# A residual quantiser between two convolutions: one add, the turned one-hots, the updates and the code choice done in another way

## The chip, the cores and the metric

The kernel runs on one core of one Trainium2 chip. The metric is the device time of one execution in microseconds (us), the median of several runs. Five engines work side by side, each in the order in which its instructions were written, and wait for each other by semaphores: PE (matrix multiply), DVE (vector), ACT (activation), POOL, and SP, which issues transfers. Transfers run on 16 DMA engines that all queues share.

## The reference

The input x has B=2 sequences of T=16000 tokens with D=512 channels in bf16. The reference convolves along time with three taps per channel, applies SiLU, quantises with four codebooks of eight words each, and convolves the quantised signal again:

```python
z = sum over i of xp[:, i:i+T, :] * dw_enc[i]
z = silu(z)
res, q = z, 0
for s in range(4):
    cb = codebooks[s]                      # 8 words of 512
    d2 = |res|^2 - 2 res.cb^T + |cb|^2
    sel = cb[d2.argmin(-1)]                # the first of equal words
    q, res = q + sel, res - sel
y = sum over i of qp[:, i:i+T, :] * dw_dec[i]
```

## The kernel before

**Tiles.** The 32000 tokens are 128 partitions of S=250 consecutive tokens each. A group g is the 128 tokens at place g of every partition. The groups are cut into 16 chunks, SIZES (line 25): one of 12, fourteen of 16, one of 14. In a chunk, the channels lie on the partitions in KT=4 blocks of 128, and the tokens of up to 16 groups on the free axis, so that a full tile is 128x2048.

**Front** (load, lines 348 to 381; front, lines 383 to 467). Chunk 0 is read as rows and turned by PE; every other chunk is read by 18 transposing transfers from SP, one per group with a neighbour on each side (line 358), into one of two XT buffers. For each of the four channel blocks, DVE makes three products (product, line 410: Z, T, T), adds them in two steps (total, line 418), then SiLU is exp (ACT, line 422), plus one (DVE, 426), log (ACT, 430), exp (ACT, 433), and a product into RES (DVE, 438). There are 3 Z and 3 T buffers; Z is held from the first product to line 438. In total and add_up (lines 413 and 443) a branch for k <= DMA_ADDS issues the add as an accumulating DMA from POOL instead; DMA_ADDS is 0, so it is not taken.

**Stage s of 4** (stage, lines 469 to 621). PE scores: per bank of up to 6 groups, a mask and 8 small matmuls a group (lines 489 and 494) leave in PSUM the products of each token with the words and with all tokens; DVE takes the largest of the masked diagonal as the norm (502) and copies the dot products (505). Six small DVE steps choose the word: with_norm (522), distance (528), least (532), marks (536, which words equal the least), first (541, the greatest of the marks weighted by preset ranks in KEY, line 271), and onehot (549). PE turns the one-hots by four transposes (turn, 559) and ACT copies them to OHT (turned, 566). Then RES is updated: for each of the four channel blocks and each pair of quarters j, j+1 of the chunk, either PE selects the words (SEL, 584) and DVE adds them (subtract, 596), a quarter of 512 columns at a time, or PE sums RES and the words (NEW, 601 and 584) and ACT copies 1024 columns back (keep, 607). ON_DVE (line 28) says how many of the four blocks go to DVE in stages 0 to 2: 1, 1, 2, and 2, 2, 3 in the last three chunks. Stage 3 updates nothing.

**Finish** (lines 664 to 692). The second convolution is matmuls of OHT with words already multiplied by the taps (Y, 633), copied by ACT (639) to YSB and stored from SP (643), four groups at a time.

**PSUM.** Of the eight banks, the pool psG has two (scores), psD two single ones (SEL), psA two double ones (NEW, Y, the turned one-hots and set-up work).

**The order.** No engine chooses at run time. Plan (line 40) takes every step with its engine, an assumed time on the engine (hold), a time to its result (delay), what it needs, a due time and the buffers that it takes and gives back. It plays the steps through once while the program is built: on each assumed engine, of the steps that are ready and have their buffers, the one due first is emitted. That fixes the order on every engine. Chunks are due 56 assumed us apart per 16 groups (PERIOD), the stages of one chunk 0.9 of that apart, the blocks of a front 0.3. SP's loads are assumed to hold 1.4 and land after 2.2; an add by DMA to hold 1.2 + 1.8 f and land after 7.5, f being the chunk's size over 16. The stores are planned on an engine of their own, OUT, but in the program they stand in SP's queue among the loads. Where PE would be idle, a warming matmul (line 313) is put in.

Of the kernel before, what the change touches and what calls it, by code (L numbers as in the profile page):

```python
# [18 lines left out]
GC = 16  # L19
J = 4  # L20
GB = 6
HT = 64
# [97 lines left out]
def kernel(  # L120
# [61 lines left out]
    for i in range(KT):  # L182
# [4 lines left out]
    plan = Plan({"XT": 2, "Z": ZB, "T": TB, "E": EB, "LN": LNB, "Y": YB, "psG": 2, "psD": 2, "psA": 2, "RES": 3, "KEY": 3,  # L187
                 "OH": 3})

    RESB = []  # L190
# [34 lines left out]
    def code_norms():  # L225
        ONES = const.tile([NC, P], BF16, name="ONES")
        nc.vector.memset(ONES, 1.0)
        JUNK = const.tile([NC, D], BF16, name="JUNK")
        GF = const.tile([NC, 1], F32, name="GF")
        nc.vector.tensor_tensor_reduce(out=JUNK, in0=CB4[0:NC, :], in1=CB4[0:NC, :], scale=1.0, scalar=0.0,  # L230
                                       op0=ALU.mult, op1=ALU.add, accum_out=GF)
        GBB = const.tile([NC, 1], BF16, name="GBB")
        nc.vector.tensor_copy(GBB, GF)
        GBF = const.tile([NC, 1], F32, name="GBF")
        nc.vector.tensor_copy(GBF, GBB)
        DIAG = const.tile([NC, NC], BF16, name="DIAG")
        nc.vector.tensor_scalar(out=DIAG, in0=IDENT[0:NC, 0:NC], scalar1=GBF, scalar2=None, op0=ALU.mult)
        psg = psD.tile([P, 512], F32, name="ps_g", tag="psd")
        nc.tensor.matmul(psg[:, 0:NC], lhsT=ONES, rhs=DIAG, start=True, stop=True)
        nc.vector.tensor_copy(GPOS, psg[:, 0:NC])  # L240


    MASK = const.tile([P, GB, HT], BF16, name="MASK")
# [23 lines left out]
        free["OH"].append(t)  # L267

    def presets(n):
        for c in range(C):  # L270
            nc.vector.memset(KEYS[n][1][:, :, c, 0], float(C - c))
        nc.vector.memset(OHB[n], 0.0)

    KEYS, OHB = list(free["KEY"]), list(free["OH"])

# [16 lines left out]
        nc.vector.tensor_tensor(out=t, in0=t, in1=CB4, op=ALU.mult)  # L292

    early = -4.0 * PERIOD
    codes = [plan.add("DVE", 0.3, 0.5, [], early, code_words)]
    codes[0] = plan.add("DVE", 1.2, 1.4, codes, early + 2.0, lambda: code_columns(RESB[0]))
    scored = [plan.add("DVE", 2.4, 2.6, [], early + 1.0, mask), plan.add("DVE", 1.9, 2.1, [], early + 1.0, code_norms)]
# [50 lines left out]
    def load(st, org):  # L348
        g0, G, GP = st["g0"], st["G"], st["GP"]
        done = []  # L350
        if g0 == 0:
            load_rows(st, org)
            return

        def one(n):
            if n == 0:
                st["XT"] = xpool.tile([P, KT, GC + 2, P], BF16, name="XT")
# [23 lines left out]
        st["loaded"] = [done[-1], st.get("edge")]  # L381

    def front(st, org):
        n, G, MB = st["n"], st["GP"], st["MB"]
# [18 lines left out]
        def block(i):  # L403
# [44 lines left out]
            hold, delay = dve(0.67), dve(0.67) + 0.1  # L448
            z = plan.add("DVE", hold, delay, st["loaded"], due, lambda: product(0), take=("Z",))
            t = plan.add("DVE", hold, delay, st["loaded"], due, lambda: product(1), take=("T",))  # L450
            z = add_up(1, [z, t])
            t = plan.add("DVE", hold, delay, st["loaded"], due, lambda: product(2), take=("T",), give=("XT",) if i == KT - 1 else ())
# [16 lines left out]
    def stage(st, s, due):  # L469
# [53 lines left out]
                                    op=ALU.add)  # L523

        def distance():
            u["D2"] = small.tile([P, GC, C], BF16, name="D2")
            g2 = GPOS[:, C * s:C * s + C].rearrange("p (o c) -> p o c", o=1).to_broadcast([P, G, C])
            nc.vector.tensor_tensor(out=u["D2"][:, 0:G, :], in0=u["V"][:, 0:G, :], in1=g2, op=ALU.add)

        def least():  # L530
            u["M"] = small.tile([P, GC], BF16, name="M")
            nc.vector.tensor_reduce(out=u["M"][:, 0:G], in_=u["D2"][:, 0:G, :], axis=AX.X, op=ALU.min)

        def marks():
            u["KEY"] = free["KEY"].pop(0)
            nc.vector.tensor_tensor(out=u["KEY"][1][:, 0:G, :, 1], in0=u["D2"][:, 0:G, :],
                                    in1=u["M"][:, 0:G].to_broadcast([P, G, C]), op=ALU.is_equal)

        def first():
            u["M2"] = small.tile([P, GC], F32, name="M2")  # L540
            nc.vector.tensor_reduce(out=u["M2"][:, 0:G], in_=u["KEY"][0][:, 0:G, :], axis=AX.X, op=ALU.max)

        def onehot():
            if s == 0:
                st["OH"] = free["OH"].pop(0)
            dst = st["OH"][:, 0:G, s, :].rearrange("p (m j) c -> p j m c", j=J)
            key = u["KEY"][0][:, 0:G, :].rearrange("p (j m) c -> p j m c", m=MB)
            best = u["M2"][:, 0:G].rearrange("p (j m) -> p j m", m=MB).to_broadcast([P, J, MB, C])
            nc.vector.tensor_tensor(out=dst, in0=key, in1=best, op=ALU.is_equal)
            free["KEY"].append(u["KEY"])  # L550
            if s == Nq - 1 and G > st["G"]:
# [12 lines left out]
        def turned():  # L564
            u["OHT"] = ohpool.tile([P, GC // J, P], BF16, name="OHT", tag="oht" if s < Nq - 1 else "fin")
            nc.scalar.activation(u["OHT"][:, 0:MB, :], u["ps"][:, 0:W].rearrange("p (m t) -> p m t", t=P), ACT.Copy)  # L566
            st["OHT"] = u["OHT"]

        due += 0.01 * PERIOD
        t = plan.add("DVE", 0.2, 0.33, maxima, due, with_norm)  # L570
        t = plan.add("DVE", 0.15, 0.26, [t], due, distance)
        t = plan.add("DVE", 0.2, 0.33, [t], due, least)
        t = plan.add("DVE", 0.2, 0.33, [t] + preset[0:3], due, marks, take=("KEY",))
        t = plan.add("DVE", 0.2, 0.33, [t], due, first)
# [12 lines left out]
        def tokens(i, j, count):  # L587
            return st["RES"][:, i, 2 * j * MB:2 * (j + count) * MB, LC:LC + HT]

        def chosen(i, j):  # L590
            u["SEL", i, j] = psD.tile([P, 512], F32, name="SEL", tag="psd")
            select(u["SEL", i, j][:, 0:W], i, j, True)

        def subtract(i, j):
            old = tokens(i, j, 1)
            nc.vector.tensor_tensor(out=old, in0=old, in1=u["SEL", i, j][:, 0:W].rearrange("p (m t) -> p m t", t=HT), op=ALU.add)  # L596

        def rest(i, j):
            NEW = u["NEW", i, j] = psA.tile([P, 2, 512], F32, name="NEW", tag="psa")
# [3 lines left out]
                select(NEW[:, h, 0:W], i, j + h, False)  # L603

        def keep(i, j):
            old = tokens(i, j, 2).rearrange("p (h m) t -> p h m t", h=2)
            nc.scalar.activation(old, u["NEW", i, j][:, :, 0:W].rearrange("p h (m t) -> p h m t", t=HT), ACT.Copy)  # L607

        due += 0.01 * PERIOD
        for j in range(0, J, 2):  # L610
            for i in range(KT):
                if i < on_dve[s]:
                    for k in (j, j + 1):
                        c = plan.add("PE", 0.25 * f, 0.25 * f + 0.2, [t, words], due, lambda i=i, k=k: chosen(i, k), take=("psD",))
                        st["new"][i, k] = plan.add("DVE", 0.1 + 0.53 * f, 0.2 + 0.53 * f, [c] + seen, due,
                                                   lambda i=i, k=k: subtract(i, k), give=("psD",))
# [117 lines left out]
```

## Time and profile before

| | us |
|---|---|
| median of 3 runs | 830.86 |
| the runs | 828.19, 830.86, 836.56 |
| span of the profiled execution (first to last instruction) | 824.6 |
| its own time | not given beside the span; the median is 6.3 above it |
| busy PE, DVE, ACT, POOL in it | 653.2, 752.2, 717.8, 7.4 |
| DMA engines busy, mean share by the SP queue | 35.8% |
| granted PE clock, mean | 0.912 |

One execution is profiled; busy times are unions of the engine's instructions. A group's line in the profile gives the line of the kernel, the engine, the operation, what it writes and reads with shapes, the count, the busy time of the group, the mean duration of one in ns, and the idle time of the engine just before, with what ended it. Instructions of one engine overlap at their ends, so that the mean duration is longer than the distance from one start to the next.

### The profile page before, as it was taken

How to read it: one execution, taken by the hardware profiler on the slowest of the kernel's cores; microseconds unless marked ns; L12 is line 12 of the kernel's file. 1: busy time of each engine (PE TensorE's matmuls, PEld its weight loads, DVE VectorE, ACT ScalarE, POOL GpSimd, SP SyncE). 2: the span in 40 equal slices, each digit the busy share in tenths (PEclk: the TensorE clock that was granted, in tenths of full speed). 3: DMA queues.
4: the chain of work that ended last, by engine and by line, in shares of the span. 5: the costliest groups of instructions: out<-in, count | busy, mean ns of one | idle time of the engine just before them, and what ended most of it. 6: DMA issues, size and time to landing. Idle time of an engine off the chain costs nothing.

```text
span 824.6 us, 23407 instructions
## 1 busy us (share of the span) xinstructions
PE 653.2 (79%) x10289; PEld 314.0 (38%) x10289; DVE 752.2 (91%) x1584; ACT 717.8 (87%) x623; POOL 7.4 (1%) x17
## 2 busy tenths in 40 slices
PE   3047697898788879868888788779898888989995
PEld 2023333443343444424444244334434434334442
DVE  5987999999999999999999999998989999988871
ACT  2659788898999999999999999998989999886564
POOL 1100000000000000000000000000000000000000
PEclk9566877798998999999999999998979999989998
DMA  7442422152452635253716353451615301111132
GB/s 172 48 98 61 86 52 59 34 117 39 109 111 53 136 70 99 59 119 72 160 53 148 59 117 72 89 138 42 135 44 110 98 36 70 52 79 52 79 143 114
DMA packets 156207, 71.82 MB, mean 87 GB/s; under 512 B 147401, under 2 KB 147786, under 8 KB 155978
## 3 DMA queue, kind: packets, MB, share of 16 engines
q1 hardware_dynamic: 155152, 69.64, 35.8%
q8 instruction: 80, 1.31, 0.7%
q0 software_dynamic: 672, 0.43, 0.5%
q10 hardware_dynamic: 282, 0.26, 0.1%
q14 instruction: 21, 0.17, 0.1%
HBM read 2.39 MB, written 32.77 MB: 43 GB/s over the span
## 4 chain that ended last, share of the span: by engine, by line
ACT 41%; DVE 31%; PE 22%; issue 3%; DMA 2%; ACTq 0%; DVEq 0%
ACT RES L607 11%; ACT LN L430 8%; ACT YSB L639 7%; ACT E L422 7%; ACT E L433 7%; DVE Z L418 6%; DVE RES L596 6%; PE PS L494 6%; PE NEW L601 5%; DVE TR L502 4%; DVE RES L438 3%; DVE T L410 3%; PE NEW L584 3%; PE Y L633 3%; PE SEL L584 2%
## 5 line engine op out<-in xcount | busy, mean ns | idle before, releaser
L607 ACT ACTIVATE RES<-NEW 128x1024 bf16<-128x1024 f32 (+1 forms) x238 | 234.7, 1037 | 29.2 <-PE NEW L584 24.6
L494 PE MATMUL PS<-RES 128*64 128x80 bf16 (+1 forms) x8064 | 189.3, 208 | 27.4 <-DVE RES L438 26.7
L596 DVE TENSOR_TENSOR RES<-RES,SEL 128x512 bf16<-128x512 bf16 (+1 forms) x292 | 185.7, 674 | 19.6 <-PE SEL L584 19.2
L494 PEld LDWEIGHTS <-RES 128*64 128x64 bf16 x8064 | 165.6, 119 | 75.5 <-issue 36.8
L601 PE MATMUL NEW<-RES,IDENT 128*128 128x512 bf16 (+1 forms) x476 | 154.2, 408 | 30.8 <-ACT RES L607 27.0
L418 DVE TENSOR_TENSOR Z<-Z,T 128x2048 bf16<-128x2048 bf16 (+1 forms) x128 | 153.7, 1200 | 0.0
L639 ACT ACTIVATE YSB<-Y 128x1024 bf16<-128x1024 f32 (+1 forms) x126 | 128.1, 1042 | 17.8 <-PE Y L633 12.0
L422 ACT ACTIVATE E<-Z 128x2048 bf16<-128x2048 bf16 (+1 forms) x64 | 122.6, 1916 | 16.2 <-DVE Z L418 16.2
L430 ACT ACTIVATE LN<-E 128x2048 f32<-128x2048 bf16 (+1 forms) x64 | 122.3, 1913 | 8.0 <-DVE E L426 8.0
L433 ACT ACTIVATE E<-LN 128x2048 bf16<-128x2048 f32 (+1 forms) x64 | 122.8, 1920 | 0.2
L502 DVE TENSOR_REDUCE TR<-PS 128x5 bf16<-128x320 f32 (+1 forms) x188 | 95.5, 510 | 17.9 <-PE PS L494 17.5
L633 PE MATMUL Y<-A,OHT 128*128 128x512 bf16 x249 | 86.4, 390 | 30.5 <-ACT RES L607 17.2
L584 PE MATMUL SEL<-OHT,CBN 32*128 32x512 bf16 (+1 forms) x292 | 84.4, 397 | 27.3 <-ACT OHT L566 15.5
L584 PE MATMUL NEW<-OHT,CBN 32*128 32x512 bf16 (+1 forms) x476 | 97.8, 407 | 0.0
L410 DVE TENSOR_SCALAR T<-XT,WENC 128x2048 bf16<-128x2048 bf16 (+1 forms) x128 | 93.5, 740 | 0.0
L584 PEld LDWEIGHTS <-CBN 32*128 32x128 bf16 x768 | 35.2, 92 | 149.9 <-issue 144.4
L438 DVE TENSOR_TENSOR RES<-Z,E 128x2048 bf16<-128x2048 bf16 (+1 forms) x64 | 76.9, 1202 | 6.6 <-ACT E L433 4.0
L601 PEld LDWEIGHTS <-IDENT 128*128 128x128 bf16 x476 | 33.7, 99 | 106.0 <-issue 103.8
L489 PE MATMUL PS<-MASK,IDENT 128*128 128x320 bf16 (+1 forms) x188 | 62.6, 333 | 10.4 <-DVE PR L505 10.1
L633 PEld LDWEIGHTS <-OHT 128*128 128x128 bf16 x373 | 32.5, 98 | 70.2 <-issue 46.9
L566 ACT ACTIVATE OHT<-ps_oh 128x512 bf16<-128x512 bf16 (+1 forms) x64 | 39.7, 623 | 17.0 <-PE ps_oh L559 16.9
L633 PE MATMUL Y<-B,OHT 128*128 128x512 bf16 x124 | 47.4, 383 | 0.1
(73 smaller groups left out, 370.9 us busy)
## 6 DMA issues: line engine op xcount, KB each, us to landing
out_dram<-YSB SPq DMA_DIRECT2D x61, 512.0 KB, 3.2
XT<-in_x_dram SPq DMA_TRANSPOSE x267, 2.8
RES<-in_x_dram SPq DMA_DIRECT2D x1, 1664.0 KB, 6.9
out_dram<-YSB SPq DMA_DIRECT2D x1, 384.0 KB, 2.3
out_dram<-YSB SPq DMA_DIRECT2D x1, 256.0 KB
A<-in_dw_dec_dram POOLq DMA_DIRECT2D x2, 96.0 KB, 5.3
CB<-in_codebooks_dram ACTq DMA_DIRECT2D x1, 128.0 KB
A<-in_dw_dec_dram POOLq DMA_DIRECT2D x2, 64.0 KB, 4.8
```

The source lines that it names most:

```text
L418: nc.vector.tensor_tensor(out=z, in0=z, in1=t, op=ALU.add)
L422: nc.scalar.activation(u["E"][:, 0:G, :], u["Z"][:, 0:G, :], ACT.Exp, scale=-1.0)
L430: nc.scalar.activation(u["LN"][:, 0:G, :], u["E"][:, 0:G, :], ACT.Ln)
L433: nc.scalar.activation(u["E"][:, 0:G, :], u["LN"][:, 0:G, :], ACT.Exp, scale=-1.0)
L494: nc.tensor.matmul(V[h * HT:(h + 1) * HT, r, :], lhsT=half[:, LC:LC + HT], rhs=half[:, lo:hi], start=False, stop=(i == KT - 1), skip_group ...
L502: nc.vector.tensor_reduce(out=u["TR"][:, q:q + m], in_=u["V", q][:, :, own:own + HT], axis=AX.X, op=ALU.max)
L584: nc.tensor.matmul(ps, lhsT=CBN[s][rows, i * P:(i + 1) * P], rhs=u["OHT"][rows, 0:MB, :], start=start, stop=True, skip_group_check=True)
L596: nc.vector.tensor_tensor(out=old, in0=old, in1=u["SEL", i, j][:, 0:W].rearrange("p (m t) -> p m t", t=HT), op=ALU.add)
L601: nc.tensor.matmul(NEW[:, h, 0:W], lhsT=IDENT, rhs=tokens(i, j + h, 1), start=True, stop=False, skip_group_check=True)
L607: nc.scalar.activation(old, u["NEW", i, j][:, :, 0:W].rearrange("p h (m t) -> p h m t", t=HT), ACT.Copy)
L633: nc.tensor.matmul(Y[:, h, :], lhsT=lhs(), rhs=rhs, start=(a == 0), stop=(a == len(terms) - 1))
L639: nc.scalar.activation(u["YSB"][:, k:k + n, :], u[k][:, 0:n, :], ACT.Copy)
```

## The change

Four things are altered; the sizes, the chunks, ON_DVE and the due times stay.

1. **First add by DMA.** DMA_ADDS becomes 1. The first of the two adds of each block (z = Z + T1) is issued from POOL as a DMA that accumulates T1 into Z, 512 KB for a full block; the second stays on DVE and waits for it.
2. **One-hots turned by DMA.** In all chunks but the last (BY_PE = 1), a transposing DMA from SP reads OH and writes OHT; PE's transposes and ACT's copy are gone there. SP's loads no longer follow each other in a chain, their assumed times become 1.31 and 2.9, and the XT buffer is given back only after all products have been made.
3. **1024-wide updates.** DVE's update takes two quarters in one instruction from a double bank. psD is gone; psA has three double banks, which SEL, NEW, Y and the rest share.
4. **Words of distance and rank.** KEY's 32-bit word gets the distance in bf16 as its upper half, and as its lower half a bf16 made of (distance < 0) minus the rank c/8. One minimum over the words as f32 finds the first nearest word; onehot compares with it. The steps are with_norm, distance, ranks, least, onehot. The 24 presets of KEY are gone, and eight small memsets on POOL make RANK.

```diff
-DMA_ADDS = 0
+DMA_ADDS = 1
+BY_PE = 1
...
-    psD = ctx.enter_context(tc.tile_pool(name="psD", bufs=2, space=bass.MemoryType.PSUM))
-    psA = ctx.enter_context(tc.tile_pool(name="psA", bufs=2, space=bass.MemoryType.PSUM))
+    psA = ctx.enter_context(tc.tile_pool(name="psA", bufs=3, space=bass.MemoryType.PSUM))
...
+        room = plan.add("SP", 0.0, 0.0, [], org - 2.2 * PERIOD, place, take=("XT",))
         for n in range(G + 2):
...
-            t = plan.add("SP", 1.4, 2.2, done[-1:], due, (lambda n=n: one(n)) if inside else (lambda n=n: edge(n)),
-                         take=("XT",) if n == 0 else ())
+            t = plan.add("SP", 1.31, 2.9, [room], due, (lambda n=n: one(n)) if inside else (lambda n=n: edge(n)))
...
         def distance():
...
-            nc.vector.tensor_tensor(out=u["D2"][:, 0:G, :], in0=u["V"][:, 0:G, :], in1=g2, op=ALU.add)
+            nc.vector.tensor_tensor(out=u["KEY"][1][:, 0:G, :, 1], in0=u["V"][:, 0:G, :], in1=g2, op=ALU.add)
+
+        def ranks():
+
+            word = u["KEY"][1]
+            nc.vector.scalar_tensor_tensor(out=word[:, 0:G, :, 0], in0=word[:, 0:G, :, 1], scalar=0.0,
+                                           in1=RANK.to_broadcast([P, G, C]), op0=ALU.is_lt, op1=ALU.subtract)
 
         def least():
...
+            u["M"] = small.tile([P, GC], F32, name="M")
+            nc.vector.tensor_reduce(out=u["M"][:, 0:G], in_=u["KEY"][0][:, 0:G, :], axis=AX.X, op=ALU.min)
...
+        def across():
+            u["OHT"] = ohpool.tile([P, GC // J, P], BF16, name="OHT", tag="oht" if s < Nq - 1 else "fin")
+            nc.sync.dma_start_transpose(out=u["OHT"][:, 0:MB, :], in_=st["OH"][:, 0:G, :, :].rearrange("p g s c -> p (g s c)"))
+            st["OHT"] = u["OHT"]
...
-        t = plan.add("PE", 0.05 + 0.06 * MB, 0.25 + 0.06 * MB, [t], due, turn, take=("psA",), give=("OH",) if s == Nq - 1 else ())
-        t = plan.add("ACT", 0.2 + 0.3 * f, 0.32 + 0.3 * f, [t], due, turned, give=("psA",))
+        if st["n"] < len(chunks) - BY_PE:
+            t = plan.add("SP", 1.31, 3.0, [t], due - 4.0 * PERIOD, across, give=("OH",) if s == Nq - 1 else ())
+        else:
+            t = plan.add("PE", 0.05 + 0.06 * MB, 0.25 + 0.06 * MB, [t], due, turn, take=("psA",), give=("OH",) if s == Nq - 1 else ())
+            t = plan.add("ACT", 0.2 + 0.3 * f, 0.32 + 0.3 * f, [t], due, turned, give=("psA",))
...
         def subtract(i, j):
-            old = tokens(i, j, 1)
-            nc.vector.tensor_tensor(out=old, in0=old, in1=u["SEL", i, j][:, 0:W].rearrange("p (m t) -> p m t", t=HT), op=ALU.add)
+            old = pair(tokens(i, j, 2))
+            nc.vector.tensor_tensor(out=old, in0=old, in1=u["SEL", i, j][:, :, 0:W].rearrange("p h (m t) -> p h m t", t=HT), op=ALU.add)
...
                 if i < on_dve[s]:
-                    for k in (j, j + 1):
-                        c = plan.add("PE", 0.25 * f, 0.25 * f + 0.2, [t, words], due, lambda i=i, k=k: chosen(i, k), take=("psD",))
...
+                    c = plan.add("PE", 0.3 * f, 0.3 * f + 0.2, [t, words], due, lambda i=i, j=j: chosen(i, j), take=("psA",))
+                    st["new"][i, j] = st["new"][i, j + 1] = plan.add("DVE", 0.1 + 1.06 * f, 0.2 + 1.06 * f, [c] + seen, due,
+                                                                     lambda i=i, j=j: subtract(i, j), give=("psA",))
```

More of the change, by code (lines that the diff above doesn't have):

```diff
@@ L186 @@
     free = {"RES": [], "KEY": [], "OH": []}
-    plan = Plan({"XT": 2, "Z": ZB, "T": TB, "E": EB, "LN": LNB, "Y": YB, "psG": 2, "psD": 2, "psA": 2, "RES": 3, "KEY": 3,
+    plan = Plan({"XT": 2, "Z": ZB, "T": TB, "E": EB, "LN": LNB, "Y": YB, "psG": 2, "psA": 3, "RES": 3, "KEY": 3,
                  "OH": 3})
@@ L237, in code_norms @@
         nc.vector.tensor_scalar(out=DIAG, in0=IDENT[0:NC, 0:NC], scalar1=GBF, scalar2=None, op0=ALU.mult)
-        psg = psD.tile([P, 512], F32, name="ps_g", tag="psd")
-        nc.tensor.matmul(psg[:, 0:NC], lhsT=ONES, rhs=DIAG, start=True, stop=True)
-        nc.vector.tensor_copy(GPOS, psg[:, 0:NC])
+        psg = psA.tile([P, 2, 512], F32, name="ps_g", tag="psa")
+        nc.tensor.matmul(psg[:, 0, 0:NC], lhsT=ONES, rhs=DIAG, start=True, stop=True)
+        nc.vector.tensor_copy(GPOS, psg[:, 0, 0:NC])
     MASK = const.tile([P, GB, HT], BF16, name="MASK")
@@ L269, in presets @@
     def presets(n):
-        for c in range(C):
-            nc.vector.memset(KEYS[n][1][:, :, c, 0], float(C - c))
         nc.vector.memset(OHB[n], 0.0)
-    KEYS, OHB = list(free["KEY"]), list(free["OH"])
+    OHB = list(free["OH"])
+    RANK = const.tile([P, 1, C], BF16, name="RANK")
+    for c in range(C):
+        nc.gpsimd.memset(RANK[:, :, c], c / C)
     PARTS = {}
@@ L294 @@
     early = -4.0 * PERIOD
-    codes = [plan.add("DVE", 0.3, 0.5, [], early, code_words)]
+    codes = [plan.add("DVE", 0.3, 0.5, [], early, code_words, take=("psA",), give=("psA",))]
     codes[0] = plan.add("DVE", 1.2, 1.4, codes, early + 2.0, lambda: code_columns(RESB[0]))
-    scored = [plan.add("DVE", 2.4, 2.6, [], early + 1.0, mask), plan.add("DVE", 1.9, 2.1, [], early + 1.0, code_norms)]
+    scored = [plan.add("DVE", 2.4, 2.6, [], early + 1.0, mask), plan.add("DVE", 1.9, 2.1, [], early + 1.0, code_norms, take=("psA",), give=("psA",))]
     preset = [plan.add("DVE", 0.8, 1.0, [], early + 2.0 if n == 0 else 0.1 * PERIOD, lambda n=n: presets(n)) for n in range(3)]
@@ L353, in load, with place @@
             return
+        def place():
+            st["XT"] = xpool.tile([P, KT, GC + 2, P], BF16, name="XT")
         def one(n):
-            if n == 0:
-                st["XT"] = xpool.tile([P, KT, GC + 2, P], BF16, name="XT")
             nc.sync.dma_start_transpose(out=st["XT"][:, :, n, :], in_=group_rows(g0 + n - 1))
@@ L380, in load @@
                 st["edge"] = plan.add("POOL", 1.0, 1.4, [t], due, lambda n=n: shift(n))
-        st["loaded"] = [done[-1], st.get("edge")]
+        st["loaded"] = done + [st.get("edge")]
     def front(st, org):
@@ L450, in block @@
             t = plan.add("DVE", hold, delay, st["loaded"], due, lambda: product(1), take=("T",))
+            st["taps"] += [z, t]
             z = add_up(1, [z, t])
-            t = plan.add("DVE", hold, delay, st["loaded"], due, lambda: product(2), take=("T",), give=("XT",) if i == KT - 1 else ())
+            t = plan.add("DVE", hold, delay, st["loaded"] + (st["taps"] if i == KT - 1 else []), due, lambda: product(2), take=("T",), give=("XT",) if i == KT - 1 else ())
             st["taps"].append(t)
@@ L525, in distance @@
         def distance():
-            u["D2"] = small.tile([P, GC, C], BF16, name="D2")
+            u["KEY"] = free["KEY"].pop(0)
             g2 = GPOS[:, C * s:C * s + C].rearrange("p (o c) -> p o c", o=1).to_broadcast([P, G, C])
-            nc.vector.tensor_tensor(out=u["D2"][:, 0:G, :], in0=u["V"][:, 0:G, :], in1=g2, op=ALU.add)
-        def least():
[L531 to L541, printed above, removed]
+            nc.vector.tensor_tensor(out=u["KEY"][1][:, 0:G, :, 1], in0=u["V"][:, 0:G, :], in1=g2, op=ALU.add)
[3 more added lines that the diff above has]
+                                           in1=RANK.to_broadcast([P, G, C]), op0=ALU.is_lt, op1=ALU.subtract)
+        def least():
+            u["M"] = small.tile([P, GC], F32, name="M")
+            nc.vector.tensor_reduce(out=u["M"][:, 0:G], in_=u["KEY"][0][:, 0:G, :], axis=AX.X, op=ALU.min)
         def onehot():
@@ L547, in onehot @@
             key = u["KEY"][0][:, 0:G, :].rearrange("p (j m) c -> p j m c", m=MB)
-            best = u["M2"][:, 0:G].rearrange("p (j m) -> p j m", m=MB).to_broadcast([P, J, MB, C])
+            best = u["M"][:, 0:G].rearrange("p (j m) -> p j m", m=MB).to_broadcast([P, J, MB, C])
             nc.vector.tensor_tensor(out=dst, in0=key, in1=best, op=ALU.is_equal)
@@ L567, in turned @@
             st["OHT"] = u["OHT"]
+        def across():
+            u["OHT"] = ohpool.tile([P, GC // J, P], BF16, name="OHT", tag="oht" if s < Nq - 1 else "fin")
+            nc.sync.dma_start_transpose(out=u["OHT"][:, 0:MB, :], in_=st["OH"][:, 0:G, :, :].rearrange("p g s c -> p (g s c)"))
+            st["OHT"] = u["OHT"]
+            if s == Nq - 1:
+                free["OH"].append(st["OH"])
         due += 0.01 * PERIOD
         t = plan.add("DVE", 0.2, 0.33, maxima, due, with_norm)
-        t = plan.add("DVE", 0.15, 0.26, [t], due, distance)
+        t = plan.add("DVE", 0.2, 0.33, [t] + preset[0:3], due, distance, take=("KEY",))
+        t = plan.add("DVE", 0.2, 0.33, [t], due, ranks)
         t = plan.add("DVE", 0.2, 0.33, [t], due, least)
-        t = plan.add("DVE", 0.2, 0.33, [t] + preset[0:3], due, marks, take=("KEY",))
-        t = plan.add("DVE", 0.2, 0.33, [t], due, first)
         t = plan.add("DVE", 0.2, 0.36, [t], due, onehot, take=("OH",) if s == 0 else (), give=("KEY",))
-        t = plan.add("PE", 0.05 + 0.06 * MB, 0.25 + 0.06 * MB, [t], due, turn, take=("psA",), give=("OH",) if s == Nq - 1 else ())
-        t = plan.add("ACT", 0.2 + 0.3 * f, 0.32 + 0.3 * f, [t], due, turned, give=("psA",))
+        if st["n"] < len(chunks) - BY_PE:
[3 more added lines that the diff above has]
+            t = plan.add("ACT", 0.2 + 0.3 * f, 0.32 + 0.3 * f, [t], due, turned, give=("psA",))
         st["turned"] = t
@@ L588, in tokens, with pair @@
             return st["RES"][:, i, 2 * j * MB:2 * (j + count) * MB, LC:LC + HT]
+        def pair(t):
+            return t.rearrange("p (h m) t -> p h m t", h=2)
         def chosen(i, j):
-            u["SEL", i, j] = psD.tile([P, 512], F32, name="SEL", tag="psd")
-            select(u["SEL", i, j][:, 0:W], i, j, True)
+            SEL = u["SEL", i, j] = psA.tile([P, 2, 512], F32, name="SEL", tag="psa")
+            for h in range(2):
+                select(SEL[:, h, 0:W], i, j + h, True)
         def subtract(i, j):
-            old = tokens(i, j, 1)
-            nc.vector.tensor_tensor(out=old, in0=old, in1=u["SEL", i, j][:, 0:W].rearrange("p (m t) -> p m t", t=HT), op=ALU.add)
+            old = pair(tokens(i, j, 2))
+            nc.vector.tensor_tensor(out=old, in0=old, in1=u["SEL", i, j][:, :, 0:W].rearrange("p h (m t) -> p h m t", t=HT), op=ALU.add)
         def rest(i, j):
@@ L605, in keep @@
         def keep(i, j):
-            old = tokens(i, j, 2).rearrange("p (h m) t -> p h m t", h=2)
+            old = pair(tokens(i, j, 2))
             nc.scalar.activation(old, u["NEW", i, j][:, :, 0:W].rearrange("p h (m t) -> p h m t", t=HT), ACT.Copy)
```

2 lines of the change are left out of this document (removed).

## The prediction

> **What bounds the kernel now.** I read the page's busy shares first, then the stretches of the span, the groups by form, the timeline round one one-hot, and the DMA issues. From the page:
>
> ```profile
> PE 653.2 (79%) x10289; PEld 314.0 (38%) x10289; DVE 752.2 (91%) x1584; ACT 717.8 (87%) x623; POOL 7.4 (1%) x17
> ```
>
> From the stretches (columns: the stretch, its length, then busy time with instruction counts of PE, PEld, DVE, ACT, POOL, then the granted clock, the DMA share and GB/s):
>
> ```profile
> 20.00:40.00 20.00, 0.63 (x5) 0.26 (x4) 19.52 (x32) 11.97 (x9) 3.79 (x6) 0.51 0.41 47
> 40.00:60.00 20.00, 7.36 (x113) 5.15 (x114) 17.57 (x33) 10.40 (x7) 0.00 (x0) 0.67 0.48 96
> 100.00:700.00 600.00, 499.08 (x8075) 239.31 (x8076) 575.75 (x1179) 573.61 (x493) 2.01 (x4) 0.93 0.38 86
> ...
> 740.00:800.00 60.00, 57.96 (x930) 26.40 (x929) 48.03 (x118) 37.67 (x41) 0.00 (x0) 1.00 0.22 88
> ```
>
> DVE has the larger total, but from 100 to 700 us both are full: DVE 575.75 and ACT 573.61 of 600. They bind together, so a change must lighten both. Before 60 us DVE leads and ACT waits; after 740 us PE is full (57.96 of 60). PE has slack elsewhere.
>
> ```profile
> L596 DVE TENSOR_TENSOR RES<-RES,SEL 128x512 bf16<-128x512 bf16 x276 | 177.3, 681 | 15.0 <-PE SEL L584 14.6
> ...
> L418 DVE TENSOR_TENSOR Z<-Z,T 128x2048 bf16<-128x2048 bf16 x120 | 146.1, 1217 | 0.0
> ...
> L566 ACT ACTIVATE OHT<-ps_oh 128x512 bf16<-128x512 bf16 x60 | 37.9, 632 | 15.3 <-PE ps_oh L559 15.2
> ...
> L596 DVE TENSOR_TENSOR RES<-RES,SEL 128x384 bf16<-128x384 bf16 x16 | 8.4, 549 | 4.6 <-PE SEL L584 4.6
> ```
>
> These groups are what the change touches. Their means cannot be multiplied straight into a saving: neighbours on an engine overlap, and what an instruction really occupies is from its start to the next start. In the timeline the 2048-wide add begins at 57.52 and the next instruction at 58.65: 1.13, not 1.217. The 1536-wide one takes 0.87 (24.70 to 25.57), four subtractions of 512 take 2.39 in the chain of work (0.60 each), a 512-wide one-hot copy on ACT 0.48 and a 384-wide one 0.37 (60.40 to 60.77).
>
> **The change part by part.** *First add to a DMA.* 64 of the 128 L418 adds leave DVE: 60 x 1.13 + 4 x 0.87 = 71 us. In their place POOL issues 64 transfers of 512 KB, and the second add waits for each. POOL is 1% busy; the seven L288 issues took 0.55 to 0.92 us each, so its own time (about 64 x 0.9 = 58 us) lies beside everything. The landing is what matters, and no accumulating transfer is in this trace. These are the nearest rows (columns: out<-in, queue, operation, count, KB each, us to landing):
>
> ```profile
> out_dram<-YSB SPq DMA_DIRECT2D x61, 512.0 KB, 3.2
> XT<-in_x_dram SPq DMA_TRANSPOSE x267, 2.8
> ...
> A<-in_dw_dec_dram POOLq DMA_DIRECT2D x2, 96.0 KB, 5.3
> ...
> out_dram<-YSB SPq DMA_DIRECT2D x1, 128.0 KB, 1.9
> ```
>
> From SP, 384 KB more cost 1.3 us, so 512 KB are about 1.7. From POOL a small transfer takes 5.3, of which 96 KB are 0.3: 5.0 to begin with. Added to that, 512 KB moved once give 6.7, moved three times (two reads and a write that do not overlap) 10.1; I take twice, 8.4. The order is made with 7.5 us (add_up), and before, the second add started a few us after the first, so 0.9 us of lateness mostly vanishes in the wait that the order already has. I cost it at nothing after the start-up, for 6.7 to 10.1 us. Other work covers it: DVE does other blocks and stages meanwhile.
>
> [...]
>
> The start-up has no cover. Chunk 0's four blocks start exp at 27.1, 30.9, 35.0 and 41.2; with some 8 us between products and second add in place of about 1, and three Z and three T buffers, the first starts 6 to 7 us later and the fourth waits for a Z buffer, so that scoring, which needs all four, begins up to 17 us later than now. DVE is lighter there (it is at 19.52 of 20), and chunk 1's products fill some of the gap. By the same stretches ACT idled 39 us in the first 100 (8.0 and 9.6 of it in the two rows above); I add 9 us, between 0 and 17.
>
> *One-hots by DMA.* Sixty of the 64 turns leave PE and ACT (the last chunk keeps its four): on ACT 56 x 0.48 + 4 x 0.37 = 28 us; on PE 236 transposes, which costs nothing now except in stages where PE is full, and there the last chunk stays as it was. SP issues 60 more transfers of the shape of XT's (1.27 us median to issue, 2.8 to land): 76 us on a queue that now has 268 transposes and 64 stores, 268 x 1.27 + 64 x 0.33 = 361 of 825 us. It stays under 60%. Is the one-hot then late? The timeline of one stage now:
>
> ```profile
> 378.02 0.28 DVE L549 TENSOR_TENSOR OH<-KEY,M 128x128 bf16<-128x128 f32 x1
> ...
> 379.81 0.38 PE L559 MATMUL ps_oh<-IDENT,OH 128*128 128x128 bf16 x4 [0.30 <-ACT RES L607]
> ...
> 382.19 0.77 ACT L566 ACTIVATE OHT<-ps_oh 128x512 bf16<-128x512 bf16 x1
> ```
>
> From one-hot to turned copy it is 382.96 - 378.30 = 4.7 us, because the short steps queue on two full engines. Pairing all 64 L549 rows with the L566 rows in order of time, the least is 1.1 and the median 7.7 us. A DMA at 1.3 + 2.8 = 4.1 us is no later than what is there, so I cost the wait at nothing; the bounds are from 1.9 us (the smallest store) to 8.3 (the slowest XT landing), and at the upper end it is about where it is now. No turn from SBUF is in the trace.
>
> *1024-wide updates.* From 384 to 512 columns is (681 - 549)/128 = 1.03 ns a column, so 512 more make 0.60 + 0.53 = 1.13 us against 1.20: 146 x 0.07 = 10 us of DVE. Three shared double banks replace two double and two single ones. A SEL that waits for DVE may now keep a bank from ACT, or ACT lend DVE one; the waits that exist (NEW for RES on ACT 27.0, SEL for DVE 10.4 us) lie on PE, which has slack. Nothing, between -10 and +15.
>
> *Words.* Six small DVE steps become five, at about 0.20 start to start; the distance now writes strided, as L536 does (299 against 220 ns), and the rank step has two operations. Net 0.1 x 64 = 6 us off DVE, between -13 and +6. The 24 presets of L271 go: 1.6 us.
>
> *The loads.* They lose the chain from one to the next and the XT buffer waits for all twelve products; both lie on SP and DVE in the order they have. Nothing.
>
> **The sum.** DVE 752 - 71 - 10 - 6 - 2 = 663. ACT 718 - 28 = 690. ACT is now the bound alone, and the shares on DVE are not moved, so DVE's 89 us buy only what ACT now waits for. The span of the profiled execution: 824.6 - 28 = 796.6. Of ACT's 26 us idle from 100 to 700 (600 - 573.6) I take half, 13, since DVE is no longer full: 783.6; bounds 0 and 26. Plus 9 for the start: 792.6. The page gives the span and no time of its own beside it; the median of the three runs lies 830.86 - 824.6 = 6.3 above. 792.6 + 6.3 = 799 us.
>
> **The rivals.** *The accumulate lands late* (slower). In place: the second add, L418, is in DVE's order at a fixed place, and behind it queue reductions that free PS banks and subtractions that free SEL, so PE and then ACT stop too. Price: each us beyond the cover is 64 us of DVE. DVE 663 + its present idle 72 leaves 90 us to 825, so it decides from 1.4 us per block, a landing near 10 us with 7.5 planned and a little slack; at 2 us: 663 + 128 + 72 = 863 of span, less a few that overlap present idle, 860 in time. For it: the upper bound is 10.1 without any company, and the DMA share of 0.38 rises by 64 transfers. [...] Against: the second add is often taken late anyway. [...]
>
> *One-hots held in SP's line* (about no change). A store waits at SP for ACT's YSB, and what stands behind it waits too:
>
> ```profile
> SPq L643 <- ACT YSB L639: 245.2, 49, 19.6
> ```
>
> That is 245.2 us over 49 stores, the longest 19.6. If ACT falls behind DVE against the order, a one-hot ready behind such a store holds PE, and with it both update engines; at 0.5 us for each of 60, 30 us: 829. Against it: most of these waits are SP with nothing ready behind.
>
> PE is no rival: without 236/252 of L559's 25.8 us it would hold (499 - 24)/(600 - 28) = 0.83 of the shortened middle.
>
> **How the numbers follow.** Forecast case 0.58: 799, its own range 777 (796.6 - 26 + 6.3) to 820 (796.6 + 17 + 6.3). Held one-hots 0.16: 829. Late accumulates 0.26: 860. A measurement of this kernel can tell about 1% from no change, so faster than 822.5 is 0.58, within 1% 0.16, slower 0.26. The range 775 to 860 leaves out about 0.03 below and half the late case, 0.13, above.
>
> **What would show it.** Right: ACT above 95% from 100 to 700 us, DVE near 84%, L566 four times, the second add after its DMA without idle, no SEL wait above 30 us. Wrong: DVE idle before L418 released by the DMA into Z, with POOL issues above 1 us (late accumulate); PE idle at L584 released by the DMA into OHT (held one-hots); ACT idle growing by more than 17 us before 100 us (start-up mis-sized).

## The result, and the profile after

The change makes the kernel slower: 881.46 us (median of 4 runs, 876.33 to 888.26) against 830.14, a ratio of 1.0645 (95% interval 1.0601 to 1.0689). The forecast was 799, the range 775 to 860. Medians and ratios below are each from one chip with the kernel before beside it; a ratio leaves out disturbed runs, and a median does not.

The page of the changed kernel, and its stretches (columns as in the prediction):

```profile
PE 661.8 (75%) x10005; PEld 307.8 (35%) x10060; DVE 672.4 (77%) x1286; ACT 691.0 (79%) x563; POOL 66.9 (8%) x89
```

```profile
20.00:40.00 20.00, 0.28 (x2) 0.13 (x2) 15.22 (x28) 7.94 (x6) 5.98 (x8) 0.50 0.85 125
40.00:60.00 20.00, 0.55 (x4) 0.26 (x4) 14.63 (x20) 15.38 (x11) 3.37 (x4) 0.50 0.61 116
100.00:700.00 600.00, 482.14 (x7243) 216.38 (x7282) 471.79 (x895) 514.50 (x418) 42.86 (x47) 0.84 0.69 137
740.00:800.00 60.00, 50.10 (x877) 24.91 (x879) 54.51 (x99) 47.01 (x39) 3.12 (x3) 0.91 0.29 74
```

The work went down as forecast: ACT 691.0 (forecast 690), DVE 672.4 (663). But no engine is full any more: from 100 to 700 us ACT idles 600 - 514.5 = 85.5 us where it idled 26, DVE 128 where it idled 24, and the granted PE clock is 0.84 instead of 0.93. The waits say for whom (columns: who waited, for what, us in total, times, longest), before and after:

```profile
ACT RES L607 <- PE NEW L584: 24.6, 30, 2.9
DVE RES L596 <- PE SEL L584: 19.2, 30, 2.7
```

```profile
ACT RES L623 <- PE NEW L596: 105.2, 73, 8.1
DVE RES L612 <- PE SEL L596: 99.9, 49, 5.8
...
PE SEL L596 <- DMA OHT<-OH: 68.2, 21, 7.2
...
ACT E L427 <- DVE Z L423: 22.9, 10, 12.2
```

Both update engines wait for PE's word matmuls, 205 us together (44 before), and PE waits for the one-hots that SP brings. One such place, in the timeline of the changed kernel:

```profile
284.77 5.60 SPq L363 DMA_TRANSPOSE XT<-in_x_dram  x4
...
285.38 0.28 DVE L552 TENSOR_TENSOR OH<-KEY,M 128x128 bf16<-128x128 f32 x1
...
288.66 1.05 PE L500 MATMUL PS<-RES 128*64 128x80 bf16 x48
...
290.48 1.22 SPq L574 DMA_TRANSPOSE OHT<-OH  x1
...
296.08 0.60 PE L596 MATMUL SEL<-OHT,CBN 32*128 32x512 bf16 x2 [6.37 <-DMA OHT<-OH]
...
296.73 1.22 DVE L612 TENSOR_TENSOR RES<-RES,SEL 128x1024 bf16<-128x1024 bf16 x1 [5.76 <-PE SEL L596]
...
298.23 1.02 ACT L623 ACTIVATE RES<-NEW 128x1024 bf16<-128x1024 f32 x1 [5.08 <-PE NEW L596]
```

The one-hot is ready at 285.66. SP has four loads of XT in front of it and issues it only at 290.48; it lands 5.6 us later. The order assumed that SP is free at once or nearly so, and 3.0 us from its start to the landing; from the one-hot's end it is 10.4. PE stands for 6.37 us at the matmul that comes next in its fixed order, DVE for 5.76, ACT for 5.08. And then PE is slow (columns of the stretches):

```profile
286.00:292.00 6.00, 3.66 (x103) 2.36 (x102) 4.97 (x8) 6.00 (x6) 0.85 (x1) 1.00 0.67 137
292.00:300.00 8.00, 3.92 (x48) 1.87 (x49) 1.94 (x3) 2.17 (x2) 0.00 (x0) 0.57 0.90 193
```

The clock is 1.00 before the pause, 0.57 around its end and 0.50 in the microsecond after it. Over the 30 one-hots whose landing the trace holds, ready to landed took 4.8 us on average and 10.6 at most. The harm sits in a few of them: the eight longest of PE's 21 waits, 3.4 to 7.2 us each, make 48 of the 68.2 us, and each of these eight one-hots stood in SP's queue behind two to four loads of XT (the one being issued included), two of them behind a store too. The clock is 1.00 in the microsecond before each of the eight pauses and 0.50 in the one after it (0.75 after the shortest).

Three theories at first: **A**, PE stands before one-hots that come late, and the rest follows; **B**, the add by DMA costs by itself (late start, Z held longer, DMA engines full); **C**, SEL and NEW hold each other up in the three shared banks.

### The profile page after: what moved, and what is told of

The parts are those of the page before. It is cut to its first block, busy times and chain, and to the rows that moved or that the text cites. A ratio compares the mean times of both kernels' runs of the same rounds, so it can differ in the third digit from the quotient of the medians.

```text
span 876.8 us, 22856 instructions
## 1 busy us (share of the span) xinstructions
PE 661.8 (75%) x10005; PEld 307.8 (35%) x10060; DVE 672.4 (77%) x1286; ACT 691.0 (79%) x563; POOL 66.9 (8%) x89
## 4 chain that ended last, share of the span: by engine, by line
PE 21%; ACT 10%; DVE 9%; SPq 6%; DMA 5%; issue 2%; ACTq 0%; DVEq 0%
PE NEW L617 6%; SPq L363 6%; PE PS L500 6%; DMA OHT<-OH 4%; PE NEW L596 4%; ACT YSB L654 3%; DVE RES L612 3%; ACT LN L435 2%; PE Y L648 2%; ACT RES L623 2%; PE PS L495 2%; DVE TR L508 2%; PE SEL L596 1%; ACT E L438 1%; DVE T L415 1%
## 5 line engine op out<-in xcount | busy, mean ns | idle before, releaser
L612 DVE TENSOR_TENSOR RES<-RES,SEL 128x1024 bf16<-128x1024 bf16 (+1 forms) x146 | 171.5, 1200 | 100.0 <-PE SEL L596 99.9
L500 PE MATMUL PS<-RES 128*64 128x80 bf16 (+1 forms) x8064 | 198.1, 213 | 48.1 <-DVE RES L443 46.9
L500 PEld LDWEIGHTS <-RES 128*64 128x64 bf16 x8064 | 173.7, 122 | 92.5 <-DVE RES L443 48.0
L617 PE MATMUL NEW<-RES,IDENT 128*128 128x512 bf16 (+1 forms) x476 | 180.7, 470 | 24.6 <-ACT RES L623 10.8
L596 PE MATMUL SEL<-OHT,CBN 32*128 32x512 bf16 (+1 forms) x292 | 61.5, 455 | 88.4 <-DMA OHT<-OH 68.2
L421 POOL DMA_DIRECT2D Z<-T x64 | 59.3, 927 | 687.2 <-DVE Z L415 152.5
L596 PE MATMUL NEW<-OHT,CBN 32*128 32x512 bf16 (+1 forms) x476 | 110.6, 461 | 0.0
L415 DVE TENSOR_SCALAR T<-XT,WENC 128x2048 bf16<-128x2048 bf16 (+1 forms) x128 | 93.7, 735 | 3.3 <-DMA Z<-T 3.2
L648 PE MATMUL Y<-A,OHT 128*128 128x512 bf16 x221 | 75.5, 386 | 18.6 <-ACT YSB L654 13.0
L423 DVE TENSOR_TENSOR Z<-Z,T 128x2048 bf16<-128x2048 bf16 (+1 forms) x64 | 76.8, 1200 | 3.8 <-DMA Z<-T 3.8
L415 DVE TENSOR_SCALAR Z<-XT,WENC 128x2048 bf16<-128x2048 bf16 (+1 forms) x64 | 47.1, 737 | 0.2
```

The source lines that it names most:

```text
L415: nc.vector.tensor_scalar(out=places(u[name]), in0=taps(i, k), scalar1=WENC[:, i, k:k + 1], scalar2=None, op0=ALU.mult)
L500: nc.tensor.matmul(V[h * HT:(h + 1) * HT, r, :], lhsT=half[:, LC:LC + HT], rhs=half[:, lo:hi], start=False, stop=(i == KT - 1), skip_group ...
L596: nc.tensor.matmul(ps, lhsT=CBN[s][rows, i * P:(i + 1) * P], rhs=u["OHT"][rows, 0:MB, :], start=start, stop=True, skip_group_check=True)
L617: nc.tensor.matmul(NEW[:, h, 0:W], lhsT=IDENT, rhs=tokens(i, j + h, 1), start=True, stop=False, skip_group_check=True)
L648: nc.tensor.matmul(Y[:, h, :], lhsT=lhs(), rhs=rhs, start=(a == 0), stop=(a == len(terms) - 1))
```

## The experiments

**Parts undone.** Three kernels from the changed one:

```diff
-BY_PE = 1          # onehots_by_pe, wide_and_words
+BY_PE = 16
-DMA_ADDS = 1       # add_on_dve, wide_and_words
+DMA_ADDS = 0
```

> All one-hots turned by PE and copied by ACT again; the other three parts stay. Theory A (PE stands in its fixed order before one-hots that come late by DMA, 68 us of PE idle at the SEL matmuls, and ACT and DVE starve behind it): 800 to 820 us, the PE wait at L596 for the one-hot below 20 us, granted clock back above 0.88. Theory B (the add by DMA costs: late start, Z held longer, DMA engines full): about 865. Theory C (SEL and NEW in three shared banks hold each other up): about 865.

Measured: 826.09 us, ratio 0.9888 (0.9835 to 0.9941) and a clock of 0.869, not above 0.88, in the profiled execution. By the median it is only 0.1% below the kernel before.

> The first add is back on DVE; one-hots by DMA, wide updates and words stay. DMA engines lose 22% of load. Theory A: 865 to 880 us, since the one-hots still come by DMA, only a little earlier. Theory B: 825 to 840. Theory C: 865 to 880.

Measured: 822.57 us, ratio 0.9939 (0.9901 to 0.9976).

> Only the 1024-wide updates from three shared banks and the words of distance and rank are left of the change. Theories A and B: the kernel before with DVE some 18 us lighter, 815 to 828 us. Theory C: slower than before, 850 or more, with waits of PE for SEL and NEW banks.

Measured: 828.06 us, ratio 0.9962 (0.9916 to 1.0007). So A comes near the first run (826 for 800 to 820) and misses the second, and B the other way round (823 for 825 to 840): either DMA step alone costs nothing, and only both together cost 55 us or more. C fails. The sum of PE's waits does not give the loss by itself: add_on_dve, which loses nothing, has 42.2 us of them, and its one-hots land 4.2 us after they are ready on average (25 landings), not much sooner than the 4.8 of the change. The issues of add_on_dve with this wait, and then the issues of the changed kernel, show where the two could meet (us from issue to landing at the end of an issue's line):

```profile
XT<-in_x_dram SPq DMA_TRANSPOSE x267, 2.8
...
OHT<-OH SPq DMA_TRANSPOSE x60, 2.3
```

```profile
PE SEL L596 <- DMA OHT<-OH: 42.2, 21, 7.6
```

```profile
Z<-T POOLq DMA_DIRECT2D x60, 512.0 KB, 5.4
XT<-in_x_dram SPq DMA_TRANSPOSE x267, 3.6
...
OHT<-OH SPq DMA_TRANSPOSE x60, 3.2
```

Two new theories: **D**, they meet on the DMA engines; **E**, they meet in the order that is fixed at build time.

**The order kept, the load on the DMA engines cut.**

```diff
-                    nc.gpsimd.dma_start(out=z, in_=t, accum_op=ALU.add)
+                    nc.gpsimd.dma_start(out=z[:, 0:2, :], in_=t[:, 0:2, :], accum_op=ALU.add)
```

> The changed kernel, its order unaltered, but each accumulating DMA adds only the first 256 of 2048 columns (seven eighths of the first add are left out), so that the DMA engines lose some 20 points of load. Each of the two DMA steps alone cost nothing (822 and 826 us), both together 55 us. Theory D (they meet on the DMA engines: with the accumulates beside them the one-hots land at 3.2 instead of 2.3 us and loads at 3.6 instead of 2.8, and PE waits): 820 to 840 us, one-hots landing at 2.3 to 2.5. Theory E (they meet in the order that is fixed at build time, which with both packs stages closer than the chip can follow): 865 to 885, with one-hots landing early and PE, ACT and DVE idle as before.

Measured: 834.89 us, ratio 1.0103 (1.0047 to 1.0160). One-hots land at 2.3 us, and PE's waits for them at SEL are half:

```profile
PE SEL L596 <- DMA OHT<-OH: 33.9, 17, 4.7
```

As D has it: without a single step moved, 47 us are gone. The lighter adds themselves and the loads land sooner too (3.0 and 2.9 us), so this is the worth of the load on the DMA engines as a whole.

**The order kept, PE's wait taken away.**

```diff
+            u["OHT"] = st["OHT"] = DEC["A0"].rearrange("p (m t) -> p m t", t=P)
             if s == Nq - 1:
                 free["OH"].append(st["OH"])
```

> The changed kernel, its order unaltered and all its transfers in place, but PE reads a constant tile of decoder words where it would read the one-hots that came by DMA, so it never waits for those transfers (the quantisation is left out in all chunks but the last). If PE's waits for one-hots, with the slower clock that follows them, are the whole harm (theory A with D as their cause): 790 to 825 us, granted clock 0.89 or more. If the order or other lateness (loads, adds, banks) makes most of it: 845 to 875.

Measured: 819.12 us, ratio 0.9834 (0.9744 to 0.9923), with all transfers still there and the one-hots landing no sooner (3.6 us). Theory A holds: what PE waits for there is worth 881 - 819 = 62 us, more than the loss of 51. The clock is 0.871 in the profiled execution, below the 0.89 expected. The edit takes one thing more away: SP no longer waits until PE has read a one-hot's buffer, in the changed kernel 27 us in 30 waits of at most 2.5, so a part of the 62 may be that. The waits of this kernel:

```profile
ACT RES L624 <- PE NEW L597: 39.9, 39, 3.5
...
DVE RES L613 <- PE SEL L597: 33.5, 23, 3.6
```

**The order made with other numbers.** planned_6us alters one number, replanned three:

```diff
-            t = plan.add("SP", 1.31, 3.0, [t], due - 4.0 * PERIOD, across, ...
+            t = plan.add("SP", 1.31, 6.0, ...       # planned_6us; replanned has 1.5, 6.0
-            t = plan.add("SP", 1.31, 2.9, [room], ...
+            t = plan.add("SP", 1.5, 4.0, [room], ...       # replanned
-                    c = plan.add("PE", 0.3 * f, 0.3 * f + 0.2, ... chosen
+                    c = plan.add("PE", 0.5 * f, 0.5 * f + 0.2, ...       # replanned, sel_half
```

> The changed kernel with one number of the order altered: a one-hot by DMA is assumed to land 6.0 us after its start, not 3.0 (traced from the end of the one-hot to its landing: 5.3 on average). If theory A holds because the order puts PE's matmuls too early, PE gets other work in front of them and the time falls to 835 to 855 us, with the PE wait for the one-hot below 30 us. Theories B and C: unchanged, 875 to 890.

Measured: 857.14 us, ratio 1.0337 (1.0276 to 1.0397). That lies in neither range, 2 us above A's; PE waits 38.8 us for one-hots, not below 30. (The average of 5.3 us in this expectation is 4.8 over the landings that the trace holds.)

> The changed kernel with one number of the order altered: PE's pair of SEL matmuls is assumed to hold PE for 0.5 us, as two single ones did before, not 0.3. Theory E, with this number as the cause (29 us of PE work are missing in the order): 835 to 860 us. Theory D: unchanged, 870 to 890.

Measured: 896.57 us, ratio 1.0844 (1.0766 to 1.0922): a miss for both theories, slower with the truer number.

> The changed kernel with the numbers of the order set to what the trace shows: SEL pair 0.5, a one-hot by DMA 1.5 on SP and 6.0 to its result, a load 1.5 and 4.0. Theory E: 820 to 840 us. Theory D: the latency is planned for but stays, 850 to 860, as with 6.0 alone (857).

Measured: 831.72 us, ratio 1.0036 (0.9999 to 1.0074). One-hots still take 4.6 us from ready to landed, but PE's wait for them at SEL is 19.1 us: PE is given other work in front. D and E look like two ends of one thing, transfers that are later than the order assumes. That making them earlier cures it, light_adds shows in an unaltered order. That telling the order cures it is likely but not shown: replanned alters three numbers at once, of which one alone gains 24 us (planned_6us) and one alone loses 15 (sel_half), and a new order can be worth tens of us for no such reason (loads_only, below).

**Which one-hots.** One condition more in the change: `s == Nq - 1 and`.

> Only the one-hots of stage 3, whose readers are the second convolution and not an update of the same chunk, come by DMA; those of stages 0 to 2 are turned by PE. Theory A as amended (the harm is PE waiting for a one-hot that the chunk's own next stage needs): 815 to 828 us, no worse than with all by PE (826). If any one-hot by DMA harms beside the accumulates: 835 to 850.

Measured: 830.43 us, ratio 1.0046 (1.0008 to 1.0084), a little above the 815 to 828 of theory A and below the other: one-hots that no update waits for do little harm, and no good.

**Why nothing is gained either.** With PE never waiting for one-hots it is 819, not 799. Theory F: PE, at a lowered clock (from 100 to 700 us 0.93 before, 0.84 in the change, 0.87 in replanned), has become the third bound.

```diff
-WARM = 0.6                            # replanned_warm, from replanned
+WARM = 0.95
-ON_DVE = ((1, 1, 2), (2, 2, 3))       # replanned_on_dve, pe_on_dve
+ON_DVE = ((1, 2, 2), (2, 2, 3))
```

> The replanned kernel (831.7 us, clock 0.87) with WARM at 0.95 instead of 0.6: the order puts in a warming matmul wherever PE is assumed idle. Theory F (the lighter DVE and ACT bring nothing because PE, at half clock after each pause, has become the third bound): clock 0.91 or more and 812 to 825 us. If PE's clock is only a symptom: 828 to 840, with the clock up or not.

Measured: 838.23 us, ratio 1.0058 (1.0013 to 1.0103), clock 0.909. (Half clock after each pause is more than the trace of the change shows: 0.50 after seven of PE's eight longest waits for one-hots, but 1.00 after one of 2.9 us.)

> The replanned kernel with ON_DVE ((1, 2, 2), (2, 2, 3)): one block more of stage 1 goes to DVE in the first 13 chunks, which takes some 24 us off ACT and 13 us off PE (two matmuls with the identity per pair fewer) and adds 29 us to DVE (674 to 703). Theory F: 810 to 825 us. If neither ACT nor PE bounds it any more but the waits of the stages for each other: 825 to 840.

Measured: 837.58 us, ratio 1.0071 (1.0029 to 1.0114).

> The same shift of one block to DVE in the kernel with the add by DMA and all one-hots by PE (826 us): 800 to 815 us by theory F and by ACT's load (715 to 690); 822 to 835 if the stages' waits for each other set the time.

Measured: 825.84 us, ratio 0.9962 (0.9923 to 1.0002). F finds no support: the clock rose (0.861 to 0.880 in the runs of replanned, 0.902 to 0.930 in those of replanned_warm) and the time did not fall, and 22 us less on ACT bought nothing. It isn't refuted outright, since each of the three kernels has an order of its own, and theory H below says what that can do.

**The parts one at a time.** narrow_after is the change without part 3, words_and_add that with BY_PE = 16, words_only that with DMA_ADDS = 0 as well; wide_only is the kernel before with part 3. Theory **G**: pairing and sharing eat what the lighter DVE gives.

```diff
-            old = pair(tokens(i, j, 2))
+            old = tokens(i, j, 1)
...
-    psA = ctx.enter_context(tc.tile_pool(name="psA", bufs=3, space=bass.MemoryType.PSUM))
+    psD = ctx.enter_context(tc.tile_pool(name="psD", bufs=2, space=bass.MemoryType.PSUM))
+    psA = ctx.enter_context(tc.tile_pool(name="psA", bufs=2, space=bass.MemoryType.PSUM))
```

> The changed kernel with the updates 512 wide from two single banks again, beside two double ones (part 3 undone alone; the order is made anew). Theory A with D (late one-hots beside accumulates): 865 to 885 us, the waits of PE for the one-hot 55 us or more. If the shared double banks carry part of the loss (theory C): 835 to 860.

Measured: 890.13 us, ratio 1.0777 (1.0684 to 1.0870), with 84.2 us of PE's waits for one-hots at SEL, a little slower than expected. The shared banks do not carry the loss.

> The kernel before with part 3 alone: 1024-wide updates from three shared double banks. By the prediction's step DVE loses 10 us and the time 0 to 10: 818 to 830 us. If the sharing and the pairing eat what the lighter DVE gives (theory G): 828 to 840, with waits of DVE's reductions for the scores of 40 us or more (17.5 before).

Measured: 832.92 us, ratio 1.0076 (1.0043 to 1.0108), in G's range; DVE's reductions wait 36.7 us for the scores, not 40 or more.

> The kernel before with part 4 and the new order of the loads alone: DVE some 8 us lighter, 816 to 828 us. If any new order of this program loses what a part gives, 828 to 840.

Measured: 851.53 us, ratio 1.0307 (1.0210 to 1.0403), slower than either range.

> The kernel before with the add by DMA and the words, without wide updates and with all one-hots by PE: DVE 65 us lighter, ACT as before. By the prediction's reasoning (ACT waits for DVE half of its idle time) 815 to 825 us; theory G has it 5 us or more faster than the same with wide updates (826); if ACT's load alone sets the time, 826 to 834.

Measured: 842.68 us, ratio 1.0178 (1.0101 to 1.0255), slower than all three ranges. G fails: with the new loads, the kernels with wide updates are 16 to 23 us faster than those without (842.68 to 826.09, 851.53 to 828.06); with the old loads they are 6 slower. Each of these has an order of its own, so a part's worth can't be read from one pair of them.

**The order alone.** The kernel before with the change's planning of the loads only:

```diff
-            t = plan.add("SP", 1.4, 2.2, done[-1:], due, ...
+            t = plan.add("SP", 1.31, 2.9, [room], due, ...
```

> The kernel before with only the change's planning of the loads (no chain between them, 1.31 and 2.9 assumed, XT kept to the last product): every engine has the same instructions as before, in an order made anew. Theory H (each order made anew is worth tens of us either way, more than the small parts themselves): about as slow as words_only, 840 to 860 us. If the words of distance and rank were what cost words_only 25 us: 822 to 832.

Measured: 858.77 us, ratio 1.0352 (1.0283 to 1.0420). The page of this kernel:

```profile
PE 671.1 (78%) x10227; PEld 317.9 (37%) x10294; DVE 756.7 (88%) x1584; ACT 720.2 (84%) x623; POOL 6.7 (1%) x17
```

ACT and DVE have the counts of before (623 and 1584) and its busy time within 5 us, and the kernel is 3.5% slower. Theory **H** holds here: an order made anew can cost tens of us by itself. words_only, at 1.0307 with an interval that overlaps, needs no cost of the words to explain it.

> The add by DMA with all one-hots by PE (826 us, 0.9888 of before) and the order made with traced numbers: a load 1.5 and 4.0, the SEL pair 0.5, an add by DMA landing after 6.0. If truer numbers help wherever transfers meet: 805 to 820 us. By theory H, anything from 815 to 845.

Measured: 829.63 us, ratio 1.0003 (0.9967 to 1.0038). Truer numbers did not help where PE turns the one-hots; the range of theory H was too wide to test it.

Of the kernels that leave nothing out, the fastest are onehots_by_pe (ratio 0.9888), add_on_dve (0.9939) and pe_on_dve (0.9962), each with one of the two DMA steps undone. All three lie within 2% of the kernel before; a gain worth having is not shown for any.

## Why the prediction was wrong

- **Busy time: right.** ACT 691.0 for 690; DVE 672.4 for 663; the two-engine reading of the page was sound.
- **First add to a DMA: right as to its own wait, and something was left out.** It lands after 5.4 us (3.9 to 7.6) where I took 8.4; the second add waits 3.8 us in total and a product 3.2. That the cost came out at nothing although the landing lies below my lower bound of 6.7 is no merit of that sum. The rival in which the add lands late had 0.26 and is refuted. One sign that I had named for it, POOL issues above 1 us, is in the trace all the same: 14 of the 15 issues in whose first 0.7 us a TENSOR_SCALAR or COPY of DVE begins (mostly L415 or L431) take POOL 0.95 to 1.55 us, 12 of them more than 1, and the other 49 take 0.84 to 0.86. What holds POOL there, the trace does not show. Here it was too little to make the second add wait more than those 3.8 us. What I left out is what these transfers do to the others: with seven eighths of their bytes gone, 47 us are gone (light_adds). ACT's busy time in the first 100 us fell from 60.9 to 52.6, near the 9 I charged for the start.
- **One-hots by DMA: the step that failed.** I set 4.1 us against a median of 7.7 now and costed the wait at nothing. (Landings count from the start of the issue, so the 4.1 holds SP's 1.3 twice; the right figure, 2.8, only strengthens the wrong conclusion.) But 7.7 us was a time that the old order planned for. Plan can be played with its assumed times alone, without the chip: in the kernel before it puts PE's first reader 8.4 us after the end of the one-hot (median), in the change 4.1, since it lets SP take the one-hot within 1.3 us and land it after 3.0. On the chip, one-hots that came late behind loads then hold PE, and DVE and ACT behind it: 68.2 us of PE's waits, and 62 us of the kernel's time, PE's lowered clock included (0.827 in the change, 0.871 in unread_onehots). What counts is lateness against the order, not against the kernel before. I also took SP's issue of 1.27 us and a landing of 2.8 from an execution in which no accumulates ran beside; beside them a one-hot lands after 3.2 us (2.3 without), a load after 3.6 (DMA share 0.38 to 0.69 from 100 to 700 us). The sign that I had named for it, PE idle at SEL released by the DMA into OHT, is what the trace shows.
- **The rival of held one-hots** (0.16, 829 us) was right in kind, with half the size and in the main the wrong place: loads of XT stand before the late ones, and only now and then a store; the clock also falls with each of PE's eight longest pauses (1.00 in the microsecond before, 0.50 or, after the shortest, 0.75 in the one after).
- **The loads: "Nothing" was wrong** in the kernel before, by 32 us, since their numbers remake the whole order (loads_only); what they cost inside the change, no run shows. Nor did the sum hold that a lighter ACT shortens the middle: ACT is 86% busy there, not above 95%, 819 is the best case measured, and moving more work off ACT did not help.
- **From span to time:** the 6.3 us that the sum adds are in the main the difference between two executions. The profiled execution of the change lasted 878.64 us with a span of 876.8, so the difference within one execution is 1.8 there.
- **Banks, words:** the shared banks are not a cause. The words' 6 us could not be told from no change.

Open: why 62 us follow from waits of which add_on_dve has 42 without a loss, why the best case is 819 and not 799, and why sel_half is slower with a truer number. Of the 32 us of loads_only, the order itself has about half: played with its assumed times alone it ends at 823.9 us, the order before at 809.3; the rest is open. An order repaired by hand, or one-hots issued where no loads stand before them, was not tried.

## What to carry to other kernels

In a kernel whose order is fixed at build time, a step that is later than the order assumes can stop the engines behind it (one one-hot here, landed 10.4 us after its end with 3.0 assumed from its start, held PE for 6.37): compare what a step takes on the chip, beside all its new neighbours, with the number assumed for it. Two sets of transfers that are each harmless can be harmful together (ratios 0.9888 and 0.9939 with one of the two, 1.0645 with both), so try such parts one by one and in pairs. And any edit to an assumed cost is a new order (1.0352 in loads_only): run the same instructions in the new order alone before crediting or blaming a part.

## What the runs showed of the hardware

An accumulating transfer of 512 KB from SBUF to SBUF issued by POOL lands after 5.4 us (median) and takes POOL 0.85; of all 64 issues, four of them of 384 KB, 14 of the 15 in whose first 0.7 us a TENSOR_SCALAR or COPY of DVE begins take 0.95 to 1.55. One of 64 KB lands after 3.0 (light_adds). A transposing transfer of 128x512 bf16 from SBUF lands after 2.3 us with no accumulates (add_on_dve) and 3.2 beside those of 512 KB; from DRAM 2.8 and 3.6.
